# List order that counts dependent neighbours on ScalarE and VectorE, with re-tuned keys and two weight loads exchanged

## The chip, the cores and the metric

One core of one Trainium2 chip. The metric is the device time of one execution in microseconds (us), the median of several. The span in a profile is some 1.8 us shorter than the time of the same execution.

Names of engines as in the profile: PE is TensorE, PEld its weight loads, ACT ScalarE, DVE VectorE, POOL GpSimd, SP SyncE.

## The reference

An attention step between tokens x and a small state runs in both directions, its two outputs are concatenated, and a feed-forward layer with a squared relu follows. Cut to what matters:

```python
# x: (8, 8, 512, 64), state: (8, 8, 32, 64)
scores = scale * x @ state^T          # softmax over the 32 states
xread  = softmax(scores) @ state
scores2 = scale * state @ x^T         # softmax over the 512 tokens
sread  = softmax(scores2) @ x
x = concat([xread, sread], axis=2)    # 544 rows for each of 8 batches, 512 wide
h = x @ w_in                          # 512 -> 2048
g = s * maximum(h, 0)**2 + b
out = g @ w_out                       # 2048 -> 512, float32
```

## The kernel before

The kernel is built as a list of operations. Each has an engine, a key (its rank, the smaller the sooner), needs, results and buffers. A small simulation at build time, `Plan.order`, gives each operation a start. The list sorted by those starts is then issued, and each engine works through its own part of the list **in that order**. So the order of two neighbours on an engine is decided here, by estimated times, and not on the chip. An operation is a candidate from `since` on:

```python
def settle(i):
    own = set(ops[i][0])
    since[i] = max(
        [ops[i][8]]
        + [ready[n] + (0.0 if own == {made_on.get(n)} else self.hop) for n in ops[i][3]]
    )
```

A result of another engine costs 0.2 us more (`hop`); a result of the same engine costs nothing more. The change begins there. The operations that the argument touches:

```python
# batch 0 and 1: M = state^T applied to w_in; wi[c] is a quarter of w_in
def M_mm(b, c): ...                    # PE, tiled, two PSUM banks; cast on ACT or DVE
    mm(ps[g][...], st_T(b, g, q, g), wi[c][64 * g : 64 * g + 64, q, :], tp=(64 * g, 32 * q))
# ... cut ...
def D_mm(b, g):                        # PE: row sums of E, then Ln, Exp, product
    A[b][f"D{g}"] = att_ps([P, S], FP32, f"D_{b}_{g}")
    mm(A[b][f"D{g}"], bones16, A[b]["E"][g])
# ... cut ...
def h_mm(name, f, lhs, rhs, ntok): ... # PE: h in one of only two banks; relu on ACT (or DVE)
# ... cut ...
def pair_sums(b, j, n): ...            # DVE: pd, three steps; step 2 needs step 1
    if n == 1:                                                       # L838
        nc.vector.tensor_tensor(pd[:, :, 2], g4[:, :, 3], pd[:, :, 0], ALU.subtract)
    else:                                                            # L840
        nc.vector.tensor_tensor(pd[:, :, 3], g4[:, :, 2], pd[:, :, 2], ALU.subtract)
# ... cut ...
def weight_sum(q, n): ...              # DVE: u, four sums over wo[q] (L892 to L898)
# ... cut ...
def bias_sum(e): ...                   # PE: wsum_ps, sums over all of wo, for the bias
# ... cut ...
def rows_out(name, rr):                # DVE: drains one of the two o banks into osb (L966)
    nc.vector.scalar_tensor_tensor(t, ob[rr % 2], s_bc, bias_bc, ALU.mult, ALU.add)
# ... cut ...
SEQ = "wi0 wi1 wi2 wo0 wo1 wi3 wo2 x2 wo3 x1 x0 x3"     # order of the loads
```

Batch 0 makes its output as plain matmuls of g with wo (`o`, four tiles of 128 rows in two banks, drained by `rows_out`); later batches use the sums pd and u. Further names in the views: T are the scores of a batch on PE, E their exps on ACT, `a` the softmax product on DVE, V the state's output on PE, and stTps the transpose of the state on PE, which needs the casts `st` first.

The softmax here doesn't subtract the row's maximum and nothing guards it: scores larger than these inputs give would overflow.

## Time and profile before

| | before |
|---|---|
| median of 6 runs | 209.8 us (209.41 to 210.12) |
| span of the profile, clock | 207.9 us, 1.000 |
| PE, DVE, ACT busy | 97%, 83%, 63% |

The prediction below shows the head of the page, the stretches, and the head of PE and ACT. One more view: DVE in order of time from 47 to 50 us. The columns are start, busy time, engine, line, operation, output and input tiles, shapes and count.

```profile
47.30 0.68 DVE L829 TENSOR_TENSOR pd<-g 128x1024 f16<-128x1024 f16 x1
48.02 0.42 DVE L838 TENSOR_TENSOR pd<-g,pd 128x512 f16<-128x512 f16 x1
48.48 0.42 DVE L840 TENSOR_TENSOR pd<-g,pd 128x512 f16<-128x512 f16 x1
48.83 0.74 DVE L966 SCALAR_TENSOR_TENSOR osb<-o,sb_cols,bias_bc 128x512 f32<-128x512 f32 x1
49.49 0.68 DVE L307 CAST M<-Mps 128x512 f16<-128x512 f32 x1
```

No line shows an idle time before it. The drain of the third o tile (L966 at 48.83), for which PE stands still, is behind two pd steps that feed each other. The start-to-start time is 0.46 us from step L838 to step L840, which needs it, and 0.35 from L840 to the drain, which doesn't.

### The profile page before, as it was taken

Reading aid. Unit: us, or ns where it says so; the run is one execution under the profiler, and the core shown is the slowest. Engines: PE = TensorE matmul, PEld = TensorE weight load, DVE = VectorE, ACT = ScalarE, POOL = GpSimd, SP = SyncE. Lnnn points to the kernel's source line nnn. Section 1 sums busy time; section 2 is a strip of 40 time slices with the busy share of each in tenths; the row PEclk is TensorE's granted clock in tenths of the full one; section 3 lists DMA queues with packets and bytes.
Section 4 is the critical chain, followed back from the end, with each engine's and each line's share of the span. In section 5 each row is a group of like instructions: output and inputs, shape, how many; then the busy total and the mean of one; then the engine's idle time right before and its main releaser. Section 6 shows DMA issues by size and latency. Waiting matters only on the chain.

```text
span 207.9 us, 4900 instructions
## 1 busy us (share of the span) xinstructions
PE 201.5 (97%) x1956; PEld 133.5 (64%) x1956; DVE 172.0 (83%) x340; ACT 131.2 (63%) x291; POOL 42.4 (20%) x67
## 2 busy tenths in 40 slices
PE   7998999998999999999999999999999999999993
PEld 3832444444767777666667766776677667888882
DVE  3588997999889686799999999999997999787652
ACT  2489998715675467878865877478756884465000
POOL 0853000132512131411602150411021101200000
PEclk9999999999999999999999999999999999999999
DMA  6999999997998529757972474363013502111132
GB/s 192 303 205 203 206 211 199 143 246 155 162 210 102 140 75 171 123 129 105 145 120 95 110 119 92 79 154 83 0 50 111 102 3 57 54 50 52 52 128 76
DMA packets 44423, 26.05 MB, mean 125 GB/s; under 512 B 26480, under 2 KB 42608, under 8 KB 44400
## 3 DMA queue, kind: packets, MB, share of 16 engines
q0 software_dynamic: 14976, 15.73, 39.8%
q1 hardware_dynamic: 29136, 9.84, 25.9%
q8 instruction: 15, 0.25, 0.5%
q10 hardware_dynamic: 288, 0.16, 0.3%
q14 instruction: 8, 0.07, 0.1%
HBM read 19.43 MB, written 8.91 MB: 136 GB/s over the span
## 4 chain that ended last, share of the span: by engine, by line
PE 86%; DVE 8%; ACT 4%; issue 1%
PE o L214 45%; PE h L214 23%; PE h_sr L214 3%; PE osr L214 3%; PE Mps L214 3%; PE warm_ps L214 3%; PE xTps L214 2%; DVE g L813 2%; PE D L214 2%; ACT g L806 1%; PE V L214 1%; DVE pd L829 1%; DVE osb L966 1%; PE T L214 1%; DVE pd L838 1%; DVE pd L840 1%
## 5 line engine op out<-in xcount | busy, mean ns | idle before, releaser
L806 ACT ACTIVATE g<-h 128x512 f16<-128x512 f32 x127 | 73.0, 598 | 32.1 <-PE h L214 30.7
L214 PE MATMUL h<-a,M 128*128 128x512 f16 x256 | 71.9, 379 | 1.0 <-ACT g L806 0.7
L214 PEld LDWEIGHTS <-pd 128*128 128x128 f16 x448 | 43.0, 98 | 20.1 <-issue 0.4
L214 PEld LDWEIGHTS <-g 128*128 128x128 f16 x400 | 38.6, 98 | 18.6 <-issue 2.3
L214 PE MATMUL o<-wo,g 128*128 128x256 f16 (+1 forms) x288 | 47.5, 296 | 0.3 <-DVE osb L966 0.3
L214 PE MATMUL o<-u,pd 128*128 128x256 f16 x336 | 46.8, 273 | 0.0
L813 DVE TENSOR_TENSOR g<-g 128x1024 f16<-128x1024 f16 x64 | 44.2, 699 | 2.1 <-ACT g L806 1.6
L1074 POOL DMA_DIRECT2D out_dram<-c x24 | 16.3, 681 | 100.7 <-DVE c L1062 100.7
L214 PEld LDWEIGHTS <-M 128*128 128x128 f16 x256 | 24.7, 98 | 14.5 <-issue 3.3
L1062 DVE SCALAR_TENSOR_TENSOR c<-o,sb_cols,bias_bc 128x512 f32<-128x512 f32 x28 | 21.0, 750 | 10.1 <-PE o L214 9.5
L307 DVE CAST M<-Mps 128x512 f16<-128x512 f32 x33 | 21.7, 681 | 0.5 <-PE Mps L214 0.5
L305 ACT CAST M<-Mps 128x512 f16<-128x512 f32 x31 | 17.6, 594 | 3.5 <-PE Mps L214 3.5
L829 DVE TENSOR_TENSOR pd<-g 128x1024 f16<-128x1024 f16 x28 | 19.2, 685 | 0.2
L1062 DVE SCALAR_TENSOR_TENSOR c<-o,sb_cols,c 128x512 f32<-128x512 f32 x21 | 15.7, 748 | 4.0 <-PE o L214 3.4
L214 PE MATMUL o<-u,g 128*128 128x256 f16 x112 | 17.8, 273 | 0.0
L365 POOL DMA_DIRECT2D xn<-in_x_dram x20 | 15.7, 832 | 4.3 <-DMA wi<-in_moe_w_in_dram 4.0
L214 PE MATMUL o<-wo,pd 128*128 128x256 f16 x112 | 16.5, 273 | 0.0
L536 ACT ACTIVATE E<-T 128x256 f16<-128x256 f32 x24 | 8.9, 384 | 10.6 <-PE T L214 10.6
L840 DVE TENSOR_TENSOR pd<-g,pd 128x512 f16<-128x512 f16 x28 | 11.8, 421 | 0.5
L838 DVE TENSOR_TENSOR pd<-g,pd 128x512 f16<-128x512 f16 x28 | 11.7, 419 | 0.3
L560 ACT ACTIVATE L<-D 128x512 f32<-128x512 f32 x16 | 9.5, 594 | 1.6 <-PE D L214 1.3
L567 ACT ACTIVATE R<-L 128x512 f16<-128x512 f32 x16 | 10.1, 630 | 0.5
(81 smaller groups left out, 156.5 us busy)
## 6 DMA issues: line engine op xcount, KB each, us to landing
out_dram<-c POOLq DMA_DIRECT2D x24, 256.0 KB, 2.7
xf<-in_x_dram SPq DMA_DIRECT2D x8, 256.0 KB, 5.3
wi<-in_moe_w_in_dram POOLq DMA_DIRECT2D x4, 512.0 KB, 9.6
wo<-in_moe_w_out_dram POOLq DMA_DIRECT2D x4, 512.0 KB, 16.0
xn<-in_x_dram POOLq DMA_DIRECT2D x4, 512.0 KB, 21.2
xn<-in_x_dram POOLq DMA_DIRECT2D x16, 128.0 KB, 3.9
out_dram<-osb POOLq DMA_DIRECT2D x4, 256.0 KB, 4.8
out_dram<-c SPq DMA_DIRECT2D x4, 256.0 KB, 2.5
```

Source lines behind the costliest of these rows:

```text
L214: return nc.tensor.matmul(out, lhsT, rhs, start=start, stop=stop, tile_position=tp, is_transpose=is_transpose, skip_group_check=True,)
L305: nc.scalar.copy(dst, src)
L307: ENG[e].tensor_copy(dst, src)
L365: nc.gpsimd.dma_start(out=xn[b][:, h0:h1].rearrange("p h c d -> p h (c d)"), in_=x[b, h0:h1].rearrange("h (q c) d -> q h (c d)", q=P),)
L567: nc.scalar.activation(A[b][f"R{g}"], A[b][f"L{g}"], AF.Exp, scale=-1.0)
L806: nc.scalar.activation(g_of(name, f), OSB["h", name, f], AF.Relu)
L813: ENG[e].tensor_mul(g, g, g)
L829: nc.vector.tensor_tensor(pd[:, :, 0:2], g4[:, :, 1:2, :].to_broadcast((P, 2, 2, t)), g4[:, :, 0:4:3, :], ALU.subtract,)
L838: nc.vector.tensor_tensor(pd[:, :, 2], g4[:, :, 3], pd[:, :, 0], ALU.subtract)
L840: nc.vector.tensor_tensor(pd[:, :, 3], g4[:, :, 2], pd[:, :, 2], ALU.subtract)
L1062: nc.vector.scalar_tensor_tensor(t, src, s_bc, add, ALU.mult, ALU.add)
L1074: ENG[e].dma_start(dst[:, rows:SCH:2, hD * h : hD * h + hD], SN[b, name])
```

## The change

The intent: an operation that directly follows its own producer on ACT or DVE counts 0.1 us as not ready, so that the list puts something independent between them. The keys are tuned again for that list, and the loads of `wi3` and `wo1` are exchanged. The change was also described as moving the DMA transposes of the first two softmax tiles behind the third x; on SyncE, which issues them, the two built programs have the same order, so nothing moved there.

```diff
-    def __init__(self, caps, hop=0.2, look=0.4, solo=0.0, late=0.0):
+    def __init__(self, caps, hop=0.2, look=0.4, same=0.1, solo=0.0, late=0.0):
 ...
-                + [ready[n] + (0.0 if own == {made_on.get(n)} else self.hop) for n in ops[i][3]]
+                + [ready[n] + ((self.same if own <= {"ACT", "DVE"} else 0.0) if own == {made_on.get(n)} else self.hop) for n in ops[i][3]]
 ...
-        h1=16.1, hs=1.0, M0=-6.0, M1=4.5, T1=13.8, ...
+        h1=19.5, hs=-3.4, M0=-3.4, M1=15.0, T1=18.0, ...      (55 of 66 keys in all, cut)
 ...
-    SEQ = "wi0 wi1 wi2 wo0 wo1 wi3 wo2 x2 wo3 x1 x0 x3"
+    SEQ = "wi0 wi1 wi2 wo0 wi3 wo1 wo2 x2 wo3 x1 x0 x3"
```

More of the change, by code (lines that the diff above doesn't have):

```diff
@@ L14 @@
 class Plan:
-    def __init__(self, caps, hop=0.2, look=0.4, solo=0.0, late=0.0):
-        self.caps, self.hop, self.look, self.solo, self.late = caps, hop, look, solo, late
+    def __init__(self, caps, hop=0.2, look=0.4, same=0.1, solo=0.0, late=0.0):
+        self.caps, self.hop, self.look, self.solo, self.late, self.same = caps, hop, look, solo, late, same
         self.ops, self.pool_of, self.users = [], {}, {}
@@ L275 @@
     K = dict(
-        h1=16.1, hs=1.0, M0=-6.0, M1=4.5, T1=13.8, x2=17.3, T2=21.6, D2=23.7, M2=46.3, V0=38.1, V1=37.9, u=27.3,
-        us=-13.3, pd1=13.7, o0=25.7, o2=34.4, w=23.8, r=4.7, T=-9.2, D=10.2, Mb=5.5, V=-3.3, S=3.3, S0=-1.1,
-        E=-3.5, L=-5.8, E0=-4.8, L0=0.4, E1=-10.7, L1=-2.6, a4=-9.1, Mc=10.1, pd=19.7, solo=18.2, f0=6.0,
-        f1=17.4, mc=-12.4, hsr=-8.2, Ssr=2.8, jE00=17.6, jE01=14.7, jL00=5.7, jL01=21.9, jR00=5.9, jR01=-2.7,
-        jE10=2.7, jE11=-4.4, jL10=-8.1, jL11=-22.4, jR10=-2.0, jR11=-2.5, jM0=-1.9, jM1=6.2, xc=1.5, a2=38.2,
-        lx=9.7, la=8.1, lb=11.1, rs=29.4, xs=-1.4, x1=10.8, rL=1.3, a4L=-14.8, McL=5.6, mcL=1.9, soloL=8.6,
+        h1=19.5, hs=-3.4, M0=-3.4, M1=15.0, T1=18.0, x2=17.7, T2=21.0, D2=33.0, M2=48.2, V0=33.6, V1=36.6,
+        u=33.8, us=-12.0, pd1=10.1, o0=26.7, o2=37.8, w=23.8, r=-4.2, T=-7.4, D=10.2, Mb=5.5, V=-1.1, S=3.3,
+        S0=-1.1, E=1.7, L=-5.8, E0=0.6, L0=2.3, E1=-1.3, L1=-1.6, a4=-12.6, Mc=1.1, pd=19.5, solo=12.4, f0=-3.1,
+        f1=16.8, mc=-6.0, hsr=-4.2, Ssr=1.8, jE00=7.8, jE01=15.1, jL00=5.7, jL01=22.2, jR00=11.5, jR01=-3.7,
+        jE10=-0.4, jE11=0.0, jL10=-14.1, jL11=-5.0, jR10=-3.9, jR11=1.2, jM0=-1.5, jM1=3.1, xc=4.3, a2=38.2,
+        lx=10.0, la=7.2, lb=10.2, rs=37.2, xs=-6.8, x1=18.0, rL=1.3, a4L=-14.8, McL=1.3, mcL=1.8, soloL=8.6,
     )
```

## The prediction

> **What bounds the kernel now.** I read the page's engine table first, then the busy shares by stretch, then TensorE (PE) in order of time in the stretches where it wasn't full, and last who waited for whom there.
>
> The head of the page:
>
> ```profile
> span 207.9 us, 4900 instructions
> PE 201.5 (97%) x1956; PEld 133.5 (64%) x1956; DVE 172.0 (83%) x340; ACT 131.2 (63%) x291; POOL 42.4 (20%) x67
> ```
>
> TensorE is busy for 97% of the span, so the most that any reordering can win is small. Where the rest lies shows in the view by stretches (length, then busy time and count of PE, weight loads, DVE, ACT, POOL, then clock and DMA):
>
> ```profile
> 0.00:12.90 12.90, 11.71 (x78) 7.12 (x84) 6.52 (x20) 6.12 (x11) 6.59 (x13) 1.00 0.94 239
> 12.90:22.30 9.40, 8.35 (x90) 2.86 (x90) 8.04 (x14) 8.86 (x20) 2.52 (x3) 1.00 1.24 204
> 22.30:47.40 25.10, 25.10 (x143) 10.84 (x141) 23.03 (x51) 18.14 (x38) 3.47 (x7) 1.00 1.32 201
> 47.40:55.80 8.40, 7.83 (x127) 5.14 (x127) 7.41 (x16) 5.57 (x15) 2.73 (x6) 1.00 1.00 149
> 55.80:180.00 124.20, 124.20 (x1311) 86.07 (x1310) 109.11 (x205) 85.40 (x176) 26.43 (x39) 1.00 0.54 104
> ```
>
> From 55.8 to 180 us PE has no idle time at all. Only two stretches after the start leave room: 12.9 to 22.3, where ACT is full (8.86 of 9.40), and 47.4 to 55.8, where DVE is nearly full (7.41 of 8.40). PE in order of time in the first of them:
>
> ```profile
> 14.29 0.39 PE L214 MATMUL D<-E,bones 128*128 128x512 f16 x1
> 14.52 0.38 PE L214 MATMUL h<-a,M 128*128 128x512 f16 x1
> 15.12 0.82 PE L214 MATMUL h<-a,M 128*128 128x512 f16 x3 [0.23 <-ACT M L305]
> 15.87 0.62 PE L214 MATMUL Mps<-wi,stT 64*32 64x512 f16 x16
> 16.77 1.08 PE L214 MATMUL h<-a,M 128*128 128x512 f16 x4 [0.27 <-ACT g L806]
> 17.68 0.38 PE L214 MATMUL D<-E,bones 128*128 128x512 f16 x1
> 18.23 1.02 PE L214 MATMUL h<-a,M 128*128 128x512 f16 x4 [0.17 <-ACT g L806]
> 19.18 0.41 PE L214 MATMUL Mps<-wi,stT 64*32 64x512 f16 x8
> 19.89 1.08 PE L214 MATMUL h<-a,M 128*128 128x512 f16 x4 [0.30 <-ACT g L806]
> 20.91 0.41 PE L214 MATMUL Mps<-wi,stT 64*32 64x512 f16 x8
> 21.36 1.08 PE L214 MATMUL h<-a,M 128*128 128x512 f16 x4
> ```
>
> The starts tell more than the idle times in brackets. Four h matmuls in a row start 0.216 us apart in the full stretches (later on, x4 takes 0.86). From 14.29 to 21.36 stand 16 h, 2 D and four groups of 8 Mps that run side by side: 22 slots of 0.216, or 4.75 us, in 7.07. Each passage between tiled Mps and full-array work costs about 0.09 more (a start-to-start of 0.308 instead of 0.216), six times, 0.55 us. So about 1.8 us of PE time are lost there to waits. What it waits for is ACT, which runs this row without a gap:
>
> ```profile
> 13.38 1.21 ACT L536 ACTIVATE E<-o 128x256 f16<-128x256 f32 x4 [0.53 <-PE o L214]
> 14.45 0.62 ACT L305 CAST M<-Mps 128x512 f16<-128x512 f32 x1
> 14.91 0.65 ACT L560 ACTIVATE L<-D 128x512 f32<-128x512 f32 x1
> 15.60 0.63 ACT L567 ACTIVATE R<-L 128x512 f16<-128x512 f32 x1
> 16.14 1.07 ACT L806 ACTIVATE g<-h 128x512 f16<-128x512 f32 x2
> ```
>
> Four exps of batch 1, a cast and a Ln/Exp pair of batch 1 stand ahead of the first relu of batch 0, though only batch 0's relus free the two h banks that PE needs. The second room, at 48.9 to 50.2, is a wait for DVE:
>
> ```profile
> 49.62 0.38 PE L214 MATMUL o<-wo,g 128*128 128x256 f16 x2 [0.34 <-DVE osb L966]
> 50.22 0.39 PE L214 MATMUL D<-E,bones 128*128 128x512 f16 x1 [0.22 <-DVE M L307]
> ```
>
> By starts that is 0.50 + 0.28 = 0.78 us. All the rest is work or the fixed ends.
>
> **What the Trainium skill says.** Perfetto Trace Analysis, Identifying the Most-Contended Engine: matmul busy time is a bad measure of headroom, because matmuls are pipelined. The trace agrees: this stretch shows 1.05 us idle (9.40 less 8.35), but 1.8 us are lost by the starts. TensorE: Matmul & The Clock Gate, "Wait — 56ns, not 53.3ns?": a warm matmul of 512 columns starts 215.7 ns after the one before; the trace has 216. TensorEngine Tiling (Array Packing), Key Properties: changing the tiling mode drains TensorE; here about 0.09 us each way. VectorE: DVE Perf Modes, "The DRAIN you can't avoid": the next op doesn't start until the pipe is empty. The trace puts a size on the dependent case: the two 128x512 pd steps that feed each other start 0.46 us apart (48.02 and 48.48) with a 0.03 gap, and independent ones of that size about 0.34. That 0.12 us is what the new term in the list order (0.1) stands for.
>
> **The change part by part.** The diff changes no instruction's work. It adds 0.1 us to the readiness of an operation that follows its own producer on ACT or DVE, re-tunes the keys that rank operations, and swaps the loads of wo1 and wi3. By the order of the built program:
>
> 1. DMA. SyncE's order is the same row for row: the transposes of the first two softmax tiles stand behind the third x in both. Nothing comes from there. Only wi3 and wo1 change places on POOL's list. The waits put wo1's landing at about 23.0, wo2's at 28.6, so the sixth load lands at about 25.8. In the new order wi3 (23) is first used at about 25 by my count below, and wo1 (25.8) at about 26.3. Cost 0, with half a microsecond to spare.
>
> 2. One warm-up matmul more (19 for 18) before the first h. It fills a wait: 0.
>
> 3. Head of ACT. New order from 13.4: cast M, two exps of batch 1, cast M, relu h0, relu h1, Ln, relu h2, relu h3, Exp, relu h4, relu h5, cast M, relu h6, relu h7. The other two exps and the second Ln/Exp pair of batch 1 come only after that. One relu that DVE did (0.69 us) goes to ACT, which has one cast fewer in the head. Spacing on ACT from the trace: relu and cast about 0.49, an exp of 256 columns 0.28, Ln to Exp 0.65, Exp to the next 0.54. Worked through with the two h banks (h(n+2) waits for relu h(n)): first h at 14.30 without the 0.39 us hole for the cast (the two casts of that bank pair now run on ACT and DVE at once and end at about 14.2), relu h0 at 15.05 (before 16.14), h2 at 15.8, relu h2 at 16.55, h4 at 17.2, h6 at 18.7, relu h6 at 19.5 and relu h7 at 19.95 (before 21.18). Before, h6 started at 19.89. So PE is 1.2 us ahead here, but has still to do the second D of batch 1 (0.22), so 0.95 net.
>
> 4. From there to the sums of wo (35.14 before). ACT owes the deferred two exps, Ln and Exp (1.8 us), and four row sums E_sum of 0.76 us each, and now has less spare. Counting all PE work from 14.30 to the wo sums: 25 h pairs of 0.43 (10.8), 2 D (0.43), six Mps groups (1.3), the passages (1.1), six o groups (5.2): 18.8 us. Before took 20.85 with stTps (0.23) in it, so 1.8 us of waits. In the new order I count about 1.1: some 0.25 at h4 and 0.28 at h6, small ones, and 0.45 at h8 of batch 1, which follows h7 with no o group between while ACT finishes its row sums. Gain left: 1.8 - 1.1 = **0.7 us**.
>
> 5. At 47 to 50 us. DVE has a step of 0.34 (pd) more ahead, but the drain of the third o tile (osb) no longer stands behind two pd steps of 0.43 each: it comes about 0.5 us earlier in the queue on top of the 0.6 to 0.7 already won. That closes most of the 0.50 wait of o. But D stands two matmuls later and waits for the M cast, which keeps its place in the DVE row, so the two waits together come to about the same end. Gain here: 0 to 0.3; I take **0**.
>
> 6. Steady state, 56 to 198. T, D and h0 of batches 3 to 7 stand 0.2 to 0.9 us later in PE work, h15 at the same place. From D of the first half to h0 stays 3.5 us of PE work, as before, and ACT's path (two Ln, two Exp, and the product on DVE) is about 3.3. PE was never short here: 0 expected. Fewer dependent neighbours on DVE help only an engine that PE doesn't wait for.
>
> 7. Tail. The last small h_sr comes about 1.5 us later. The sums it feeds were ready at 196.5 and first used at 199.7: still hidden. The last 8 matmul groups, drain and output transfer are the same.
>
> Sum: 209.8 - 0.7 = 209.1; with half a chance of some of part 5, 209.0.
>
> **Rivals.** (a) All waits go: 1.8 + 0.78 = 2.6 us, 207.2. For it: somebody tuned the keys for exactly this. Against it: ACT was 94% busy in the stretch and loses little work. (b) The saved time is given back on ACT or DVE: the row sums and deferred softmax of batch 1 push the same waits to 26 to 34, or DVE, full from 39 on, decides when the o banks come free at 49; then 209.6 to 209.9. For it: DVE's 23.03 of 25.10. Against: DVE loses a 0.69 us relu before it. (c) wo1 lands later than I reckon and the o group that needs it waits: each us of it costs a us, up to 210.5. (d) The tighter h run of batches 4 to 7 (the same h within 0.9 us less of PE work) makes PE wait for relus: five batches at 0.1 to 0.3, 209.5 to 210.5. Against: ACT has 0.2 to 0.5 us gaps between relus there.
>
> **Range and chances.** Mine is 209.0; (a) bounds it below at 207.2, so over 2% faster (under 205.6) has no mechanism: 0.01. (b) to (d) reach 210.5 in bad luck; over 2% slower (above 214.0) would need several at once: 0.02. Range for 8 in 10: 208.1 to 209.9.
>
> **What would show it right or wrong.** Right: the first h at about 14.3 with no hole, relu h7 near 20, the wo sums on PE at about 34.2 with stTps behind them (35.14 less 0.23 less 0.7), no PE idle from 56 to 198, and an end 0.5 to 1 us earlier. Part 4 is wrong if PE shows no wait near 33 (then more is won) or waits of over 1 us between 21 and 34. Part 5 is wrong if the wait of D for the M cast vanishes. Part 1 is wrong if an o group waits for a DMA near 26. Parts 6 and 7 are wrong if the new stretch 55 to 180 shows PE idle.

## The result, and the profile after

| | before | after |
|---|---|---|
| median | 209.8 us (209.41 to 210.12) | 209.02 us (208.47 to 209.41) |
| ratio | | 0.9962, 95% interval 0.9942 to 0.9982 |

Ratios here and below are the mean time of one kernel's runs over that of the other's of the same rounds, so not quite the ratio of the medians quoted. The change is within 2%, and 0.8 us faster beyond the noise. The profiled execution has a span of 207.5 us; its clock of 0.998 comes from a dip in the last microsecond.

The head of the page after, and its stretches (length, then busy time and count of PE, PEld, DVE, ACT, POOL, then clock and DMA):

```profile
span 207.5 us, 4901 instructions
...
PE 201.0 (97%) x1957; PEld 133.1 (64%) x1957; DVE 170.3 (82%) x339; ACT 131.9 (64%) x292; POOL 43.4 (21%) x67
```

```profile
12.90:22.30 9.40, 8.38 (x77) 3.03 (x76) 7.12 (x14) 8.36 (x19) 2.52 (x3) 1.00 1.24 205
22.30:47.40 25.10, 24.85 (x150) 10.60 (x154) 23.14 (x50) 18.80 (x39) 4.39 (x7) 1.00 1.34 197
47.40:55.80 8.40, 8.15 (x130) 5.40 (x130) 7.36 (x17) 6.06 (x16) 3.30 (x6) 1.00 1.08 148
55.80:180.00 124.20, 124.16 (x1312) 86.38 (x1310) 108.04 (x203) 85.45 (x176) 25.95 (x38) 1.00 0.56 105
```

The head (first row), where the prediction looked for the gain, is as idle as before: PE is busy for 8.38 of 9.40 us, before 8.35. The room that has shrunk is the third: 8.15 of 8.40, before 7.83. PE in order of time shows both:

```profile
14.22 1.03 PE L214 MATMUL h<-a,M 128*128 128x512 f16 x4
...
17.21 1.06 PE L214 MATMUL h<-a,M 128*128 128x512 f16 x4
19.10 0.41 PE L214 MATMUL Mps<-wi,stT 64*32 64x512 f16 x8 [0.84 <-DMA wi<-in_moe_w_in_dram]
19.45 1.04 PE L214 MATMUL h<-a,M 128*128 128x512 f16 x4
...
34.29 0.59 PE L214 MATMUL h<-a,M 128*128 128x512 f16 x2 [0.25 <-ACT g L806]
...
48.15 1.48 PE L214 MATMUL o<-wo,g 128*128 128x512 f16 x8
49.87 0.39 PE L214 MATMUL D<-E,bones 128*128 128x512 f16 x1 [0.25 <-DVE M L307]
```

The four holes for ACT at the head are gone, as intended: h starts without one at 14.22. In their place stands one large one: the product with the third quarter of w_in waits for its transfer. The starts say 1.00 us where the bracket says 0.84 (the start before it, plus the normal 0.216, to this start; 0.09 of that is the passage to tiled work). At 49 us the wait of `o` for `osb` has gone, and only that of D remains. DVE, in the order of time, shows why:

```profile
34.88 0.43 DVE L892 TENSOR_TENSOR u<-wo 128x512 f16<-128x512 f16 x1 [0.49 <-DMA wo<-in_moe_w_out_dram]
...
39.60 1.41 DVE L966 SCALAR_TENSOR_TENSOR osb<-o,sb_cols,bias_bc 128x512 f32<-128x512 f32 x2 [0.20 <-ACT bias_bc L936]
...
47.53 0.69 DVE L829 TENSOR_TENSOR pd<-g 128x1024 f16<-128x1024 f16 x1
48.14 0.75 DVE L966 SCALAR_TENSOR_TENSOR osb<-o,sb_cols,bias_bc 128x512 f32<-128x512 f32 x1
48.80 0.41 DVE L838 TENSOR_TENSOR pd<-g,pd 128x512 f16<-128x512 f16 x1
49.13 0.68 DVE L307 CAST M<-Mps 128x512 f16<-128x512 f32 x1
```

The drain now stands between L829 and L838, which depend on each other, and step L840 has gone behind everything urgent. From 34.88 to the cast at 49.13 the view shows no idle time of DVE but the two that are marked: it waits for the last weight load (`wo3`) and, briefly, for the bias that is made from the same load. After that it is an uninterrupted row.

Where the time came from, by markers of the two traces (us from the start of the span):

| marker | before | after | ahead by |
|---|---|---|---|
| first h | 14.52 | 14.22 | 0.30 |
| h8 of batch 0 | 21.36 | 20.76 | 0.60 |
| sums of wo on PE | 35.14 | 34.81 | 0.33 |
| first drain of o on DVE | 39.70 | 39.60 | 0.10 |
| T of batch 2 on PE | 47.45 | 47.35 | 0.10 |
| third drain of o on DVE | 48.83 | 48.14 | 0.69 |
| D of batch 2 on PE | 50.22 | 49.87 | 0.35, with two o matmuls (0.22) more done |
| first V on PE | 54.59 | 54.02 | 0.57 |
| last matmul begins | 204.02 | 203.62 | 0.40 |

Of the 0.60 us at h8, 0.22 is a D still to be done, and of the 0.33 at the sums of wo, 0.23 is the four stTps matmuls, which now stand behind them. So the head's lead is 0.1 us before 40 us. Between T and V, 0.47 more appear, and one small new wait of 0.20 us, of the h at 102.18, takes some back. Each column is one profile. Over the 14 profiles the first load (wi0) already lands anywhere from 11.83 to 13.11 us, so a difference of a few tenths between two columns can be chance; T to V is a distance within one profile.

### The profile page after: what moved, and what is told of

It reads as the page before. It is cut to its first block, busy times and chain, and to the rows that moved or that the text cites. A ratio compares the mean times of both kernels' runs of the same rounds, so it can differ in the third digit from the quotient of the medians.

```text
span 207.5 us, 4901 instructions
## 1 busy us (share of the span) xinstructions
PE 201.0 (97%) x1957; PEld 133.1 (64%) x1957; DVE 170.3 (82%) x339; ACT 131.9 (64%) x292; POOL 43.4 (21%) x67
## 4 chain that ended last, share of the span: by engine, by line
PE 83%; DMA 7%; DVE 5%; POOL 1%; ACT 1%; SPq 0%; issue 0%
PE o L214 45%; PE h L214 25%; DMA wi<-in_moe_w_in_dram 6%; PE h_sr L214 3%; PE Mps L214 3%; PE osr L214 3%; DMA xf<-in_x_dram 2%; PE D L214 1%; DVE g L813 1%; PE V L214 1%; DVE pd L829 1%; DVE osb L966 1%; PE T L214 1%; POOL wi L342 1%; DVE pd L838 1%; DVE pd L840 1%
## 5 line engine op out<-in xcount | busy, mean ns | idle before, releaser
L214 PE MATMUL o<-wo,g 128*128 128x256 f16 (+1 forms) x288 | 46.7, 296 | 0.0
L813 DVE TENSOR_TENSOR g<-g 128x1024 f16<-128x1024 f16 x64 | 43.5, 692 | 3.8 <-ACT g L806 3.7
L829 DVE TENSOR_TENSOR pd<-g 128x1024 f16<-128x1024 f16 x28 | 19.6, 699 | 0.1
L840 DVE TENSOR_TENSOR pd<-g,pd 128x512 f16<-128x512 f16 x28 | 11.7, 419 | 0.4
L838 DVE TENSOR_TENSOR pd<-g,pd 128x512 f16<-128x512 f16 x28 | 11.7, 418 | 0.2
```

Of the source, the lines that this page charges most:

```text
L214: return nc.tensor.matmul(out, lhsT, rhs, start=start, stop=stop, tile_position=tp, is_transpose=is_transpose, skip_group_check=True,)
L813: ENG[e].tensor_mul(g, g, g)
L829: nc.vector.tensor_tensor(pd[:, :, 0:2], g4[:, :, 1:2, :].to_broadcast((P, 2, 2, t)), g4[:, :, 0:4:3, :], ALU.subtract,)
```

## The experiments

Two theories. **Theory H** (the head): time won or lost before 35 us goes to the end, so the hole for wi2 is what kept the change from winning more. **Theory D** (DVE's queue; not to be confused with the matmul D): DVE is held by the landing of wo3 and then is full until the drains and casts at 48 to 50, so D of batch 2 comes a fixed time after that landing (15.0 us in the new order), and the gain is only the place of the drain in that row. Each experiment moves entries of the finished list, just before it is issued; `move` takes one entry out and puts it before or behind another. All gave results within the tolerance of the comparison with the reference. Each was timed in five rounds against the kernel before.

### The hole for wi2 taken away (e1_no_wi2)

```diff
# on after
-                        wi[c][64 * g : 64 * g + 64, q, :],
+                        wi[1 if (b, c) == (0, 2) else c][64 * g : 64 * g + 64, q, :],
```

This reads the wrong quarter of w_in for one of the 32 pieces of M; the difference stays within the tolerance.

> The changed kernel, but the M product of batch 0 for the third column block reads the second weight block wi1 instead of wi2 (wrong result on purpose), so PE needn't wait for wi2 to land, at 17.9 to 19.1 us. Theory H (the hole is what ate half of the head's gain): the start-to-start hole of 1.2 us there shrinks to about 0.3, h8 starts near 20.1 instead of 20.8, T of batch 2 near 46.7 instead of 47.35, and the time falls by 0.5 to 0.7 us, to about 208.4 (0.993 of before). Theory D (DVE, gapless from the landing of wo3 at 34.9 on, decides when D of batch 2 can start at 49.9): the hole goes all the same, but PE waits again further on, D of batch 2 stays at 49.8 to 49.9, time 208.9 to 209.1, as the changed kernel.

Measured: 208.96 us, ratio 0.9978 (0.9958 to 0.9999), no better than the change itself. The hole was gone: h6 of batch 0 started 4.45 us after the first h instead of 5.23, and the sums of wo 19.99 instead of 20.59. But then PE waited 0.39 us more for stTps at 36.18, DVE waited 0.89 for wo3 (after: 0.49), and T came 32.93 us after the first h (in after: 33.13). So of 1.00 us of hole 0.2 reached T in this profile, and none is seen in the times. D of batch 2 came 15.02 us after wo3, as theory D says. Theory H in its plain form falls.

That wait for stTps is where DVE first holds PE: the casts `st` stand on DVE behind the first two sums over wo3. It shows in e0_after, the changed kernel run again (DVE, then PE):

```profile
34.38 0.43 DVE L892 TENSOR_TENSOR u<-wo 128x512 f16<-128x512 f16 x1 [0.89 <-DMA wo<-in_moe_w_out_dram]
...
35.19 0.49 DVE L307 CAST st<-stf 128x256 f16<-128x256 f32 x2
...
35.73 0.40 PE L214 MATMUL stTps<-ident,st 128*128 128x128 f16 x4 [0.24 <-DVE st L307]
```

In after, with its hole of 1.00 us, PE came to stTps just when it was ready, and T follows wo3 by 12.49 us in after, e0 and e1 alike. In e4 and e11, where wo3 landed only 19.8 and 19.7 us after the first h (20.4 to 20.6 in those three), PE didn't wait for stTps, and T came 32.56 and 32.47 us after the first h.

### The fourth row sum later (e3_rowsum_late)

The prediction had laid the wait near 34 us (h8 of batch 1) on row sums on ACT.

```diff
# on after
+    move(("sum", 1, 1), "behind", ("r", 1, 8))
+    move(("q", 1), "behind", ("sum", 1, 1))
```

> The changed kernel with the fourth row sum (and its reciprocal) moved behind the relu of h8 of batch 1, so that the PE wait of 0.42 us at 33.7 (h8 of batch 1 for a relu) goes. If waits of PE count where they stand: 0.3 to 0.4 us faster than the changed kernel, 208.6 (0.994 of before). Theory D (DVE from the landing of wo3 on decides): the wait at 33.7 goes, the same time is lost again before D of batch 2 near 49.9, and the time stays at 208.9 to 209.1 (0.996).

Measured: 209.08 us, ratio 0.9994 (0.9973 to 1.0015). The wait stayed, with the row sum out of the way, at exactly its size (0.416 us by the starts):

```profile
33.23 0.59 PE L214 MATMUL h<-a,M 128*128 128x512 f16 x2 [0.25 <-ACT g L806]
```

So the cause given in the prediction is wrong. h6, h7 and h8 stand there without other work between, and there are two h banks: h8 has to wait for the relu of h6. The experiment was clumsy as well: the reciprocal that follows the row sum now stood on DVE behind the first u sum and made DVE wait 0.49 us at 35.10, in the very row that theory D holds to be critical, after it had waited 1.49 for wo3; PE then waited 0.87 for stTps at 36.05. The matmul D came 15.40 us after wo3.

### One more pd step behind the drains (e4_pd_behind)

```diff
# on after
+    move(("pd", 1, 3, 1), "behind", ("read", 0, 3))
```

> The changed kernel with one pd step of DVE (0.42 us) moved behind the M cast and the fourth o drain at 49 us. Theory D: D of batch 2 starts at 49.6 instead of 49.9, the 0.31 us wait goes and the time falls by 0.3 us, to about 208.7 (0.9945 of before). If DVE doesn't decide here, or the moved step is missed later (at the first sums of pd near 54), nothing changes: 209.0.

Measured: 208.49 us, ratio 0.9959 (0.9941 to 0.9976). The wait of D for the cast fell from 0.42 to 0.08 us, and D came 14.97 us after wo3, no sooner than in the change's own list: in this profile L829 started 12.97 us after wo3, in after 12.67, so the row was late for another reason before it. (wo3 landed early there against the first h, so PE's own work may have set the time; that is argued, not shown.) The ratio is that of the change (0.9962). The last wait at 49 us was by then worth nothing that can be measured.

### The part at 47 to 51 us alone (e5_drain_first)

```diff
# on before
+    move(("pd", 1, 3, 1), "behind", ("read", 0, 2))
+    move(("pd", 1, 3, 2), "behind", ("read", 0, 3))
+    move(("D", 2, 0), "behind", ("s", 1, 1, 1))
```

> The kernel before with only what the change does at 47 to 51 us: the third o drain ahead of two pd steps on DVE, and D of batch 2 behind four o matmuls instead of two. The prediction's part 5 says 0 to 0.3 us, taken as 0: 209.5 to 209.8 (0.9985 to 1). What the trace of the changed kernel suggests: the waits of 0.50 and 0.28 us at 48.9 to 50.2 shrink to about 0.2 and the time falls by 0.5 us or a little more, to about 209.25 (0.997 of before), so that most of the gain of the change is this part.

Measured: 208.59 us, ratio 0.9965 (0.9945 to 0.9985): the whole gain of the change, on the old head, with the old keys and the old loads. DVE has the drain ahead of the pd steps, and PE shows no bracket there:

```profile
47.06 0.74 DVE L966 SCALAR_TENSOR_TENSOR osb<-o,sb_cols,bias_bc 128x512 f32<-128x512 f32 x1
47.72 0.41 DVE L838 TENSOR_TENSOR pd<-g,pd 128x512 f16<-128x512 f16 x1
48.05 0.69 DVE L307 CAST M<-Mps 128x512 f16<-128x512 f32 x1
```

The two waits, 0.51 and 0.38 us by the starts, became 0.08 together.

### The change again (e0_after), and its head alone (e11_head_only)

e0_after is the changed kernel as it is, a control in the second group of runs. e11_head_only undoes the part at 47 to 51 and keeps all the rest:

```diff
# on after
+    move(("pd", 1, 3, 1), "before", ("read", 0, 2))
+    move(("pd", 1, 3, 2), "before", ("read", 0, 2))
+    move(("D", 2, 0), "behind", ("s", 1, 1, 0))
```

> The changed kernel itself again, so that the other three can be held against it on the same chip and in the same rounds. 0.995 to 0.998 of before. Theory D also says that D of batch 2 starts 15.0 us after wo3 lands, whatever the landing of this execution is (15.01 in the first trace of the changed kernel, 15.02 in the one without the wi2 wait).

> The changed kernel with its part at 47 to 51 us undone (third o drain behind the two pd steps again, D of batch 2 behind two o matmuls again): what the head of the list alone is worth. Prediction's step 4: 0.7 us, 209.1, 0.9967 of before. Theory D: next to nothing, 0.998 to 1.0, with D of batch 2 about 0.5 us later than in the changed kernel against the landing of wo3 (15.5).

Measured: e0_after 208.55 us, ratio 0.9951 (0.9932 to 0.9971); wi2 happened to land at 17.90, so the hole was only 0.16 us, and D of batch 2 came 15.01 us after wo3 all the same. e11_head_only 209.59 us, ratio 1.0007 (0.9983 to 1.0031). PE waits for the drain again, for longer than before:

```profile
48.96 0.38 PE L214 MATMUL o<-wo,g 128*128 128x256 f16 x2 [0.67 <-DVE osb L966]
49.56 0.39 PE L214 MATMUL D<-E,bones 128*128 128x512 f16 x1 [0.22 <-DVE M L307]
```

The wait had been 0.51 us by the starts in before and is 0.83 here. D came 15.89 us after wo3, where 15.5 had been expected. PE came to it earlier and DVE didn't: a better head turned into a longer wait. With e5 this is shown from both sides: the part at 47 to 51 alone is the gain, and the rest of the change alone is worth nothing that the times show. From T to V it is 7.14 us in before, 6.33 in e5, 6.67 in after and e0, and 7.47 in e11. Both edits move three things at once (the drain, step L840, and D behind two more o matmuls), and no run separates them. Those two matmuls fill 0.22 us, which is an estimate of the most that moving D alone could save, of the 0.89 us of both waits in before. The runs of e11 lie 1.08 us above those of e0 on the same chip, with a 95% margin of 0.4 worked out from the six runs of each.

### DVE relieved between wo3 and the drains (e9_u_late), and with the hole away (e10_u_late_no_wi2)

If theory D is right, DVE's row must be lightened before 48 us for an earlier head to count. The sums over wo3 aren't needed until 57 us. The last three moves also bring the casts and the transpose of the state forward, so that PE doesn't wait for stTps:

```diff
# on after
+    move(("pd", 1, 3, 1), "behind", ("read", 0, 3))
+    move(("u", 3, 0), "before", ("a4", 2, 0));  move(("u", 3, 1), "before", ("a4", 2, 0))
+    move(("u", 0, 3), "before", ("g", 2, 4))
+    move(("u", 3, 2), "before", ("g", 2, 4));  move(("u", 3, 3), "before", ("g", 2, 4))
+    move(("st", 1), "before", ("q", 1))
+    move(("stps", 1), "before", ("h", 1, 8))
+    move(("stT", 2), "before", "wsum")
```

e10 is the same with the edit of e1 (wrong).

> The changed kernel with DVE relieved before 50 us: the four sums over wo3 and one over wo0 moved behind the M casts, up to 8 us later, so that DVE doesn't stand waiting for wo3 at 34 us; the state casts and transpose ahead of h8 of batch 1; and the pd step of the fourth experiment moved as well. Theory D: D of batch 2 starts without a wait and no longer 15.0 us after wo3 but 0.5 to 1 us sooner; 0.3 to 0.5 us faster than with the pd step alone, about 0.992 to 0.994 of before. If the DVE row isn't what decides: as the fourth experiment, 0.996.

> The ninth with M of batch 0, third block, reading wi1 instead of wi2 (wrong result on purpose). With DVE no longer deciding, theory D says that the hole of 0.5 to 1 us at 18 us now does count: a further 0.3 to 0.6 us, about 0.990 of before, where the same edit in the changed kernel brought nothing. If DVE is still what decides, 0 against the ninth.

Measured: e9 207.98 us, ratio 0.9934 (0.9905 to 0.9963), the fastest correct version by its median, below both kernels. In its profile D came 14.41 us after wo3 with a wait of 0.08, although the hole for wi2 was 1.05 us and wo3 landed at 35.01, the latest of all profiles. That is what theory D expects, with both holds of DVE on PE (stTps and the cast) loosened at once. As a time it is less sure: e9's runs lie 0.36 us below those of e0 on the same chip with a margin of 0.64, so that e9 beats before is shown, and that it beats the change isn't.

e10: 208.09 us, ratio 0.9931 (0.9905 to 0.9957). In its profile it is 34.56 us from the first h to D, against 35.18 in e9; the times are the same. Inconclusive. One reason may be that the hole differs between executions (0.16 in e0, 1.05 in e9), so in most of e9's runs there may be less to win than in the one that was profiled. That is argued, not shown.

### The new term off, keys new (e7_same0); old keys with the term (e6_keys_old); loads exchanged back (e2_loads_old)

```diff
# e7, on after
-    def __init__(self, caps, hop=0.2, look=0.4, same=0.1, solo=0.0, late=0.0):
+    def __init__(self, caps, hop=0.2, look=0.4, same=0.0, solo=0.0, late=0.0):
# e6, on after: the K of before
# e2, on after
+    i, j = at(("wi", 3)), at(("wo", 1))
+    steps[i], steps[j] = steps[j], steps[i]
```

> The changed kernel with the new keys and loads but without the new term (0 instead of 0.1 us for a dependent neighbour). Built, its DVE list has the two dependent pd steps next to each other again and the third o drain behind them, as in the kernel before, and D of batch 2 behind two o matmuls. Theory D: the gain is the place of that drain, so it is gone: 0.999 to 1.001 of before, with o waiting 0.5 us or more near 48. If the new keys carry the gain: 0.995 to 0.997.

> The other half: the new term and loads with the old keys. Built, DVE has one pd step and the M cast ahead of the third o drain, and the second pd step behind. By theory D the D of batch 2 waits less and the o matmuls still wait for their bank, so about half of the gain: 0.997 to 0.999 of before; but the whole order, steady state included, is one that nobody tuned, so waits elsewhere may cost up to 1 us.

> The changed kernel with wo1 loaded ahead of wi3 again, all else in place. PE comes to the third-block-plus-one product (which needs wi3) at 24.6 to 25.5 us, and as sixth load wi3 lands at 25.5 to 26.7: a hole of up to 1 us opens there. Theory D: it doesn't reach the end, 0.995 to 0.997 of before as the changed kernel. If PE's waits in the head count: 0.5 to 1 us slower, 0.998 to 1.000.

e7: 209.74 us, ratio 1.0019 (1.0002 to 1.0037). With the term at 0 the list has L829, L838, L840 and only then the drain again, both waits are back (0.37 and 0.39 us by the starts), and D came 15.61 us after wo3. The head has a hole of 0.98 at 18.30, for a cast of M on ACT that ended 0.03 us after wi2 had landed, and a new wait of 0.35 stands at 180.5. So the new keys without the term win nothing. The tie to the term is through the list: 0.1 us of unreadiness is just what lets the drain pass the dependent step.

e6: 212.33 us, ratio 1.0138 (1.0116 to 1.016), a plain miss of what was expected of it. The term moves entries in the list that the old keys had been tuned around, and PE waits in places where it never had: 0.62 us in the middle of V at 70.48, three times 0.36 to 0.40 for relus from 71.9 to 74.5, 0.57 at 78.67, besides 0.76 for a relu at 19.58. It says that term and keys belong together, and no more: that order was tuned by nobody.

e2: 209.16 us, ratio 1.0005 (0.9983 to 1.0027).

```profile
25.41 0.62 PE L214 MATMUL Mps<-wi,stT 64*32 64x512 f16 x16 [1.09 <-DMA wi<-in_moe_w_in_dram]
```

wi3 is then the sixth load, landed at 25.37, and PE stood 1.25 us for it. Here theory D doesn't hold as stated: D of batch 2 came 15.99 us after wo3 and not 15.0, T 13.66 after it (12.49 in after), and the gain was gone. So DVE's queue hides a hole at the head only up to a limit. The hole of e1 lay within it. This one made PE itself the bound at 47 us. The exchange of the loads is needed by the new order, and it costs nothing there.

### The relief on the old head (e12_before_relieved)

```diff
# on before
+    move(("pd", 1, 3, 1), "behind", ("read", 0, 3));  move(("pd", 1, 3, 2), "behind", ("q", 2))
+    move(("D", 2, 0), "behind", ("s", 1, 1, 1))
+    move(("u", 3, 0), "before", ("a4", 2, 0));  move(("u", 3, 1), "before", ("a4", 2, 0))
+    move(("u", 3, 2), "before", ("g", 2, 4));  move(("u", 3, 3), "before", ("g", 2, 4))
```

> The kernel before with the third o drain early, D behind four o matmuls, and the four sums over wo3 moved behind 50 us, so that DVE doesn't decide any more. PE then runs without a wait near 49 and what the head loses counts. Theory D: no better than the fifth experiment, 0.996 to 0.9965 of before, since there the wait of D was already down to 0.08 us; the ninth (the head of the changed kernel, DVE relieved) stays 0.3 to 0.5 us ahead of it. If the relief itself is what makes the ninth fast: 0.993 to 0.994.

Measured: 208.94 us, ratio 0.9977 (0.9958 to 0.9996); no wait left near 49, a new one of 0.26 us at 55.47. It is no better than e5, so relief of DVE without the new head isn't worth more than the drain's place. That e9 stands at 0.9934 suggests that the new head is worth some 0.4% once DVE is relieved, but the two intervals touch, they come from two groups of runs, and the two edits aren't quite the same.

### All of them

| run | on | what | median us | ratio to before | 95% |
|---|---|---|---|---|---|
| (the change) | | | 209.02 | 0.9962 | 0.9942 to 0.9982 |
| e0_after | after | again | 208.55 | 0.9951 | 0.9932 to 0.9971 |
| e1_no_wi2 | after | no hole | 208.96 | 0.9978 | 0.9958 to 0.9999 |
| e2_loads_old | after | loads back | 209.16 | 1.0005 | 0.9983 to 1.0027 |
| e3_rowsum_late | after | row sum later | 209.08 | 0.9994 | 0.9973 to 1.0015 |
| e4_pd_behind | after | L838 behind too | 208.49 | 0.9959 | 0.9941 to 0.9976 |
| e5_drain_first | before | 47 to 51 alone | 208.59 | 0.9965 | 0.9945 to 0.9985 |
| e6_keys_old | after | old keys | 212.33 | 1.0138 | 1.0116 to 1.016 |
| e7_same0 | after | term off | 209.74 | 1.0019 | 1.0002 to 1.0037 |
| e9_u_late | after | DVE relieved | 207.98 | 0.9934 | 0.9905 to 0.9963 |
| e10_u_late_no_wi2 | after | e9, no hole | 208.09 | 0.9931 | 0.9905 to 0.9957 |
| e11_head_only | after | 47 to 51 undone | 209.59 | 1.0007 | 0.9983 to 1.0031 |
| e12_before_relieved | before | DVE relieved | 208.94 | 0.9977 | 0.9958 to 0.9996 |

## Why the prediction was right or wrong

The total (209.0 for 209.02) was right, and the reasons were not: two of its steps were off by about the same amount in opposite directions. That the total came out is luck.

**Step 1, loads: right about what it looked at, blind beside it.** wo1 landed at 26.71 (25.8 was the count) and no o group waited for it. But only the exchanged loads were checked. In before, wi2 landed at 18.43 and was first used at 19.18; the prediction moved that use ahead by more than a microsecond and didn't ask again. In after it landed at 19.06, and PE had been ready at 18.10.

**Step 2, one more warm-up: cost 0, right.**

**Step 3, head of ACT: 0.95 us expected at h6, about 0.4 found at h8.** The first h came at 14.22 without a hole, as said. h6 came at 19.45 and not at 18.7, because of wi2. In e1, without that wait, h6 is 4.45 us after the first h; 4.4 had been counted. The mechanism was right and a transfer was missing in it.

**Step 4, gain left at 35 us: this is the step that failed; 0.7 us expected, 0.1 found.** The sums of wo were to start at 34.2 and started at 34.81. The waits foreseen at h4 and h6 (0.25 and 0.28) were not there; the hole for wi2 stood in their place. The wait at h8 of batch 1 was foreseen at 0.45 and was 0.42, but with a wrong cause (e3): two banks, not row sums. Neither of the signs named for this step (no wait near 33, or over 1 us of waits from 21 to 34) appeared, so they could not tell. And what the step left out weighs most: even where the hole was small (e0) or away (e1), the lead at 35 us didn't go through to 50, since DVE begins its row when wo3 lands, and PE needs that row's results, the state casts at 36 and the drain and cast at 48 to 50. Rival (b) had said that "DVE, full from 39 on, decides when the o banks come free at 49", and put 209.6 to 209.9 on it. That describes e11, the head alone: 209.59, with 209.65 for before in the same rounds.

**Step 5, 47 to 50 us: this failed as well, the other way; 0 taken, 0.5 measured between T and V in the traces, 1.1 us by the times of e11 and e0.** The prediction had seen that the drain comes about 0.5 us earlier in DVE's row. It then held that the cast "keeps its place in the DVE row" and that the two waits would add up to the same end. The cast did not keep its place: from L829 to it are 1.60 us in after (47.53 to 49.13) and 2.19 in before (47.30 to 49.49), since step L840 had gone behind it and no dependent neighbours were left in front of it. The 0.59 is 0.34 for the step and two times some 0.12 for the dependence. The wait of D didn't vanish, the sign that it had named for this step; the wait of o went, and D had two more matmuls in front of it. One reading was off as well: the wait of D in before is 0.38 us and not 0.28, since the o matmuls in front of it have 256 columns and start 0.108 apart, not 0.216; the two waits were 0.89 us together, not 0.78.

**Step 6, the steady state: nearly right.** PE is idle for 0.04 us between 55.8 and 180; by the starts one wait of 0.20 appeared, at 102.18.

**Step 7, the tail: right.** From the first V to the last matmul 149.43 us before and 149.60 after, the 0.2 just named.

**The weakness common to 4 and 5:** PE's own waits were counted in order of time, and each was taken as a gain if it went. The engine that PE waits for next was not followed back to what holds *it*. The chain of the page has the same weakness. It gives the after kernel's largest share outside of PE to the transfer of wi2, whose removal (e1) brought no time:

```profile
PE o L214 45%; PE h L214 25%; DMA wi<-in_moe_w_in_dram 6%; PE h_sr L214 3%; PE Mps L214 3%; PE osr L214 3%; DMA xf<-in_x_dram 2%; PE D L214 1%; DVE g L813 1%; PE V L214 1%; DVE pd L829 1%; DVE osb L966 1%; PE T L214 1%; POOL wi L342 1%; DVE pd L838 1%; DVE pd L840 1%
```

**What stays open:** which of the three moves at 47 to 51 us carries the gain, whether the rest of the hole for wi2 is worth anything once DVE is relieved (e10), what the new head is worth then (e12 and e9 only suggest it), why the loads land up to 1.5 us apart from one execution to the next, and what in e6's order costs the 2.9 us (1.38% of 209.28).

## What to carry to other kernels

When the busiest engine waits in two places, follow each wait back to what holds the engine it waits for: a gain ahead of a queue that starts at a fixed landing only lengthens the next wait. In an engine's row that is late rather than waiting, look at what stands in front of the urgent instruction, and put the steps nobody needs yet, above all those that feed each other, behind it. And whenever work is moved earlier, check the landing of every transfer that it reads, not only of those that the change touches.

## What the Trainium skill lacked or had wrong

- VectorE: DVE Perf Modes, "The DRAIN you can't avoid", says that the next op doesn't start until the pipe is empty, which takes roughly the op's duration less 266 ns, and that a next op that isn't held starts earlier. Here a 128x512 step with a busy time of 0.42 us is followed after 0.33 to 0.35 us by an independent one, so before its recorded end, and after 0.46 by one that needs its result. For the 128x1024 step it is 0.60 to 0.61 and 0.72. A dependent neighbour costs 0.12 us in both. No page that I found gives this figure, and the section's formula doesn't give it either: an estimate from it is 0.15 us for the step of 0.42 us and 0.41 for that of 0.68.
- TensorEngine Tiling (Array Packing), Key Properties, says that a change of the tiling mode drains TensorE, without a size: about 0.09 us each way here (0.308 from start to start for 0.216).
- Perfetto Trace Analysis, Identifying the Most-Contended Engine, warns of matmul busy time. It doesn't say that the idle times of the profile fall short too: the wait for wi2 was 0.84 us in the bracket and 1.00 by the starts, and that for the drain in e11 0.67 and 0.83. Start-to-start times are the measure.
- No page that I found says how far the landing of one and the same load moves between executions: over 14 profiles wi2 landed between 17.77 and 19.18 us and wo3 between 33.54 and 35.01, which is more than the whole effect of this change. Counted from the landing of wi0, wi2 still moves by 1.1 us (5.11 to 6.20).
